# Converting the weights in place over their raw words, with four raw buffers instead of two and two

## The chip, the core and the metric

The kernel runs on one core of a Trainium2 chip. The metric is the device time of one execution in microseconds (us), shown as a median of several runs.

## The reference

Attention with a linear bias and a window feeds two feed-forward layers. Cut to what matters:

```python
scores = scale * np.matmul(q, k.transpose(0, 1, 3, 2))      # batch 4, heads 8, seq 576, head_dim 64
scores = np.where(mask, scores + bias[None], -1000000000.0) # mask: 0 <= rel < 128
...                                                         # softmax
x = np.matmul(attn, v)          # reshaped to (2304, 512)
h = x @ w_in                    # layer 1, d_ff = 2048
g = h * np.clip(h + 3.0, 0.0, 6.0) / 6.0
x = g @ w_out
r = np.maximum(x @ w_in2, 0.0)  # layer 2, weights of its own
g = s * (r * r) + b
out = g @ w_out2
```

The four weight matrices are handed over as 64-bit floats, so each weight comes to the core as two 32-bit words, a low and a high one, side by side.

## The kernel before, in words

The 2304 tokens are eight groups (t = 0 to 7) of 256 or 320 for layer 1, and six groups (t = 8 to 13) of 384 for layer 2. The hidden dimension of 2048 is 16 slices f of 128. A `Step` (t, f) is a first product `h` (L575, 12 matmuls), an activation on ScalarE and VectorE (`relu` L588, `product` L592 or L596, `hi` L605 or L607, `lo` L612 or L614), and a second product `o` (L633 in layer 1, L647 in layer 2). Every matrix operand is kept as two parts, a rounded `hi` and a rest `lo`.

The order of the work is written by hand: `at(slot, rank, fn)` puts each piece into a slot, and all slots are issued in order, so each engine and the sync queue (SP) work through their instructions in that order. A step takes two slots.

`Half` converts the weights. There are 32 halves for each layer, two for each f: the `w_in` part and the `w_out` part. A half with slot s is

- `load` (slot s - 3): one transfer of 512 KB on the sync queue (L168) into a raw tile of 128 x 1024 words; `l` and `h` are its even and odd words, so each is a view of 512 words with a step of 8 bytes;
- `high` (slot s): ScalarE scales the high words into a PSUM bank (L181) and the low words into `q` (L182);
- `sign` (slot s): VectorE shifts the PSUM bank (L186) and joins it with the sign of `h` into `z` (L189);
- `add` (slot s + 1): GpSimd adds `z` and `q` into `q` (L195);
- `hi` (slot s + 2): ScalarE rounds `q` into the weights' tile (L203);
- `lo` (slot s + 3): VectorE writes the rest beside it (L207).

`z` and `q` are the two dense halves of a tile `zq` of 1024 words. The raw tile comes from one of two places. Either it has the tag `raw` (two buffers of 4 KB a partition, and `zq` has two more of its own, given out in `high`), or it is one half of a "stage", a tile of 2048 words in memory that is free at the time, whose other half is the `zq`. In layer 1 the stages are the tiles of the weights 12 to 15, which are filled last; in layer 2 the stage is one tile of the input pool (tag x1), with one buffer. In layer 2 the halves take two raw buffers and the stage in turn. A raw tile of the tag `raw` is last read in `sign`, a stage in `lo`. The outputs `y` of layer 1's groups use the tag `raw` too, and so does a small tile `tmp` at the start.

The halves of layer 1 are planned six slots ahead of their first use, beside the attention of the later groups, whose loads (L280, L286) stand in the same sync queue. The halves of layer 2 are planned 1.74 slots apart from six slots behind the start of t = 7, the last group of layer 1.

Of the kernel before, what the change touches and what calls it, by code (L numbers as in the profile page):

```python
# [8 lines left out]
F32 = mybir.dt.float32  # L9
F32R = mybir.dt.float32r  # L10
I32 = mybir.dt.int32
U32 = mybir.dt.uint32
AF = mybir.ActivationFunctionType
ALU = mybir.AluOpType
PSUM = bass.MemoryType.PSUM

P = 128
# [5 lines left out]
def tile_alibi_window_attention_moe_moe2(  # L23
# [14 lines left out]
    nc = tc.nc  # L38
    B, H, S, D = dims
    T, DM = out.shape  # L40
    NF = w1.shape[0]
# [4 lines left out]
    N1 = max(SIZES1)  # L46
# [5 lines left out]
    wpool = ctx.enter_context(tc.tile_pool(name="wpool", bufs=1))  # L52
    raww = ctx.enter_context(tc.tile_pool(name="raww", bufs=1))
    xpool = ctx.enter_context(tc.tile_pool(name="xpool", bufs=1))
# [6 lines left out]
    nt1 = len(SIZES1)  # L61
# [40 lines left out]
    b_sb = const.tile([P, 1], F32, name="b_sb")  # L102

    def constants():
        tmp = raww.tile([P, P], F32, tag="raw", bufs=2, name="tmp")
        nc.gpsimd.iota(own, pattern=[[-1, P]], base=0, channel_multiplier=1)
        nc.vector.tensor_copy(rel0, own)
        nc.vector.tensor_scalar(
            out=rel2[:, :P], in0=rel0, scalar1=float(P), scalar2=None, op0=ALU.add
        )  # L110
        nc.vector.memset(tmp, 0.0)
        lower = dict(compare_op=ALU.is_ge, base=0, pattern=[[-1, P]], channel_multiplier=1)
        upper = dict(compare_op=ALU.is_ge, base=-1, pattern=[[1, P]], channel_multiplier=-1)
        nc.gpsimd.affine_select(out=tmp, in_=tmp, fill=float(P), **lower)
        nc.vector.tensor_tensor(out=rel, in0=rel0, in1=tmp, op=ALU.add)
        nc.gpsimd.affine_select(out=rel0, in_=rel0, fill=BIG, **lower)
        nc.gpsimd.affine_select(out=rel2[:, :P], in_=rel2[:, :P], fill=BIG, **upper)
        nc.vector.tensor_scalar(
            out=own, in0=tmp, scalar1=-1.0 / P, scalar2=1.0, op0=ALU.mult, op1=ALU.add
        )  # L120
        make_identity(nc, ident)
        nc.sync.dma_start(out=s_sb, in_=s_in.to_broadcast([P, 1]))
        nc.sync.dma_start(out=b_sb, in_=b_in.to_broadcast([P, 1]))
# [4 lines left out]
    def bank(name):  # L128

        nonlocal nbank  # L130
        free = 4 if slot < FIRST else 2 if slot < hslot[1, 0] else 0
        nbank += 1
        k = nbank % (3 + free)
        if k < free:
            return ps_o.tile([P, 512], F32, tag=f"o{3 - k}", name=name)
        return ps_w.tile([P, 512], F32, tag="a", bufs=3, name=name)
# [4 lines left out]
    class Half:  # L141
# [17 lines left out]

        def load(self):  # L160
            if self.stage is None:
                raw = raww.tile([P, 2 * DM], I32, tag="raw", bufs=2, name=f"raw{self.id}")
            else:
                pool, tag = self.stage
                t = pool.tile([P, 4 * DM], I32, tag=tag, name=f"stage{self.id}")
                raw, self.zq = t[:, : 2 * DM], t[:, 2 * DM :]
            src = (w1 if self.layer == 1 else w2)[self.f].bitcast(I32)
            nc.sync.dma_start(out=raw, in_=src[:, 2 * self.i * DM : 2 * (self.i + 1) * DM])  # L168
            raw = raw.rearrange("p (c w) -> p c w", w=2)
            self.l, self.h = raw[:, :, 0], raw[:, :, 1]  # L170

        def high(self):

            if self.stage is None:
                self.zq = raww.tile([P, 2 * DM], I32, tag="zq", bufs=2, name=f"zq{self.id}")
            self.z, self.q = self.zq[:, :DM], self.zq[:, DM:]
            if self.layer == 1:
                self.zp = bank(f"z{self.id}")
            else:
                self.zp = ps_w.tile([P, 512], F32, tag="h", name=f"z{self.id}")  # L180
            nc.scalar.activation(self.zp, self.h.bitcast(F32), AF.Copy, scale=2.0**-112)  # L181
            nc.scalar.activation(self.q, self.l.bitcast(U32), AF.Copy, scale=2.0**-29)  # L182

        def sign(self):
            z = self.zp.bitcast(I32)
            nc.vector.tensor_scalar(  # L186
                out=z, in0=z, scalar1=3, scalar2=None, op0=ALU.logical_shift_left
            )
            nc.vector.scalar_tensor_tensor(  # L189
                out=self.z, in0=self.h, scalar=-(2**31), in1=z,  # L190
                op0=ALU.bitwise_and, op1=ALU.bitwise_or,
            )

        def add(self):
            nc.gpsimd.tensor_tensor(out=self.q, in0=self.z, in1=self.q, op=ALU.add)  # L195

        def hi(self):
            if (self.layer, self.f) not in wt:
                wt[self.layer, self.f] = wpool.tile(
                    [P, 2, 2 * DM], F32R, tag=f"w{self.f}", name=f"w{self.layer}_{self.f}"  # L200
                )
            w = wt[self.layer, self.f]
            nc.scalar.activation(w[:, 0, self.c], self.q.bitcast(F32), AF.Copy)  # L203

        def lo(self):
            w = wt[self.layer, self.f]
            nc.vector.tensor_tensor(  # L207
                out=w[:, 1, self.c], in0=self.q.bitcast(F32), in1=w[:, 0, self.c].bitcast(F32),
                op=ALU.subtract,
            )  # L210

# [3 lines left out]
    xtag = ["x0", "x1", "x2"] + [f"x{(i + 1) % 2}" for i in range(3, nt1)]  # L215
# [331 lines left out]
    class Step:  # L547
# [61 lines left out]
        def lo(self):  # L609
            hi = self.g[:, 0].bitcast(F32)  # L610
            if self.layer == 1:
                nc.vector.tensor_tensor(out=self.g[:, 1], in0=self.a, in1=hi, op=ALU.subtract)  # L612
            else:
                nc.vector.scalar_tensor_tensor(  # L614
                    out=self.g[:, 1], in0=self.a, scalar=b_sb, in1=hi,
                    op0=ALU.add, op1=ALU.subtract,
                )
# [37 lines left out]
        def end(self):  # L655
            t = self.t
            if self.layer == 1:
                if t == nt1 - 1:
                    whole = xpool.tile([P, CC, N1], F32, tag=xtag[t], name=f"y{t}")
                for e in range(0, CC, 2):  # L660
                    if t == nt1 - 1:
                        y = whole[:, e : e + 2]
                    else:
                        y = raww.tile([P, 2, N1], F32, tag="raw", bufs=2, name=f"y{t}_{e}")
                    y = y[:, :, : self.n]
                    nc.scalar.activation(y[:, 0], acc[t][e], AF.Copy, scale=1.0 / 6.0)
                    nc.vector.tensor_scalar(
                        out=y[:, 1], in0=acc[t][e + 1], scalar1=1.0 / 6.0, scalar2=None,
                        op0=ALU.mult,
                    )  # L670
                    nc.sync.dma_start(out=x2d[t][:, e : e + 2], in_=y)
                return
            for tb in range(N2 // P):
                y = late["p"].tile([P, DM], F32, tag="y2", bufs=3, name=f"y{t}_{tb}")
                if tb % 2 == 0:
                    nc.scalar.activation(y, acc[t][tb], AF.Copy)
                else:
                    nc.vector.tensor_copy(y, acc[t][tb])
                r0 = (t - nt1) * N2 + tb * P
                nc.sync.dma_start(out=out[r0 : r0 + P, :], in_=y)  # L680
# [29 lines left out]
            eng.tensor_tensor(out=x[:, 1], in0=raw, in1=x[:, 0].bitcast(F32), op=ALU.subtract)  # L710


    k = 0
    for f in range(NF):
        for i, s in enumerate((hslot[0, f], oslot[0, f])):
            room = [None] * 2 + [(wpool, f"w{i}") for i in range(max(12, f + 3), NF)]
            Half(1, f, i, room[k % len(room)]).plan(s - 6)
            k += 1
    last = hslot[nt1 - 1, 0]
    room = (None, None, (xpool, xtag[nt1 - 2]))  # L720
    for k in range(2 * NF):
        f, i = divmod(k, 2)
        s = max(last + 6 + int(1.74 * k), oslot[nt1 - 1, f])
        Half(2, f, i, room[k % 3]).plan(s)
    for u in units:
        if u.g == 0:
            u.plan(u.h)
# [15 lines left out]
    at(last, 0, late_pool)  # L743
    at(-1, 23, lambda: warm_up(5))
    at(-3, 0, constants)

    with tc.manual_schedule():
# [58 lines left out]
```

## Time and profile before

| | us |
|---|---|
| median of three runs | 970.63 |
| lowest and highest | 966.11, 972.07 |
| profiled execution | 970.56 |
| its span, first to last instruction | 968.4 |
| TensorE busy | 944.5 (98%) |
| VectorE busy | 542.8 (56%) |
| ScalarE busy | 464.4 (48%) |
| GpSimd busy | 288.1 (30%) |

PE is TensorE, DVE is VectorE, ACT is ScalarE, POOL is GpSimd, SPq is the sync queue that issues the transfers. L207 is line 207 of the kernel before. A share of the whole span is a mean over stages: layer 1 with attention (to about 500 us), the conversion of layer 2's weights (about 500 to 624 us) and the rest of layer 2.

### The profile page before, as it was taken

The page shows a single profiled execution, that of the slowest core. Times are in us where ns is not written, and L with a number is a line of the kernel's source. Part 1 is how long each engine was busy: PE and PEld are TensorE (multiplying, and loading weights), DVE is VectorE, ACT ScalarE, POOL GpSimd, SP SyncE. Part 2 cuts the span into 40 slices and gives each one's busy share as a digit, 9 for nine tenths or more (in the row PEclk, how much of TensorE's full clock was granted, in tenths as well). Part 3 has the DMA queues.
Part 4 walks back from the last instruction along what each step waited for, and adds up shares of the span by engine and source line. Part 5 has one row for each costly group of instructions (what it writes and reads, how often), then busy time and mean ns, then how long its engine had stood idle before and what let it go on. Part 6 is the DMA issues. An engine that isn't in the chain of part 4 may idle for free.

```text
span 968.4 us, 16289 instructions
## 1 busy us (share of the span) xinstructions
PE 944.5 (98%) x5978; PEld 867.7 (90%) x5978; DVE 542.8 (56%) x1334; ACT 464.4 (48%) x1201; POOL 288.1 (30%) x544
## 2 busy tenths in 40 slices
PE   8998999999999999999999999899999999999998
PEld 5688889999999999999998877799999999999997
DVE  5999995555555555455359999833323323333322
ACT  4878885555554444444247666433223323223322
POOL 5645783345544444443114533200000000000000
PEclk6599999999999999999999999999999999999999
DMA  6263542222222121220034453120110200200000
GB/s 244 82 202 118 182 154 60 94 72 96 75 93 61 56 87 61 72 84 5 1 136 163 141 175 136 66 66 1 35 31 1 66 1 1 66 0 1 34 1 33
DMA packets 34383, 73.92 MB, mean 76 GB/s; under 512 B 4352, under 2 KB 13568, under 8 KB 34304
## 3 DMA queue, kind: packets, MB, share of 16 engines
q1 hardware_dynamic: 34304, 72.89, 22.7%
q8 instruction: 47, 0.77, 0.3%
q14 instruction: 32, 0.26, 0.1%
HBM read 63.44 MB, written 9.44 MB: 75 GB/s over the span
## 4 chain that ended last, share of the span: by engine, by line
PE 77%; DVE 11%; issue 3%; DMA 3%; ACT 3%; POOL 1%; SPq 0%; POOLq 0%; ACTq 0%; DVEq 0%
PE h L575 34%; PE o L647 18%; PE o L633 15%; DVE w L207 3%; PE s L323 3%; DVE z L186 3%; PE v L406 3%; DMA stage<-w 2%; PE s L478 2%; PE t L375 2%; DVE g L612 1%; PE t L517 1%; DVE t L596 1%; ACT z L181 1%; PE v L531 1%
## 5 line engine op out<-in xcount | busy, mean ns | idle before, releaser
L575 PE MATMUL h<-x,w 128*128 128x384 f32 (+2 forms) x2688 | 446.9, 315 | 4.0 <-DVE t L592 3.7
L575 PEld LDWEIGHTS h<-x,w 128*128 128x128 f32 x2688 | 418.6, 190 | 14.3 <-DVE t L592 5.4
L588 ACT ACTIVATE t<-h 128x384 f32<-128x384 f32 (+2 forms) x224 | 99.5, 444 | 365.2 <-PE h L575 364.4
L633 PE MATMUL o<-g,w 128*128 128x256 f32 (+1 forms) x1536 | 231.6, 299 | 3.5 <-DVE g L612 1.8
L647 PE MATMUL o<-w,g 128*128 128x512 f32 x864 | 217.6, 395 | 7.1 <-ACT g L607 5.1
L633 PEld LDWEIGHTS o<-g,w 128*128 128x128 f32 x1536 | 210.0, 189 | 7.1 <-DVE g L612 3.8
L647 PEld LDWEIGHTS o<-w,g 128*128 128x128 f32 x864 | 159.8, 188 | 40.8 <-ACT g L607 7.7
L596 DVE SCALAR_TENSOR_TENSOR t<-t,s_sb 128x384 f32<-128x384 f32 x96 | 64.4, 671 | 171.5 <-ACT t L588 171.5
L391 POOL TENSOR_SCALAR_AFFINE_SELECT W<-F 128x128 f32<-128x128 f32 (+1 forms) x240 | 68.3, 323 | 145.7 <-ACT F L379 142.0
L592 DVE SCALAR_TENSOR_TENSOR t<-t,h 128x256 f32<-128x256 f32 (+1 forms) x128 | 57.7, 451 | 84.2 <-ACT t L588 84.0
L614 DVE SCALAR_TENSOR_TENSOR g<-t,b_sb,g 128x384 fp32r<-128x384 f32 x96 | 65.1, 678 | 54.1 <-ACT g L607 54.0
L612 DVE TENSOR_TENSOR g<-t,g 128x256 fp32r<-128x256 f32 (+1 forms) x128 | 72.8, 569 | 39.2 <-ACT g L605 38.2
L607 ACT ACTIVATE g<-t,b_sb 128x384 fp32r<-128x384 f32 x96 | 59.2, 616 | 65.4 <-DVE t L596 65.2
L195 POOL TENSOR_TENSOR zq<-zq 128x512 int32<-128x512 int32 x40 | 56.8, 1419 | 83.1 <-DVE zq L189 71.8
L605 ACT ACTIVATE g<-t 128x256 fp32r<-128x256 f32 (+1 forms) x128 | 55.9, 437 | 16.1 <-DVE t L592 16.0
L304 POOL TENSOR_TENSOR C<-raw,C 64x448 fp32r<-64x448 f32 (+1 forms) x48 | 50.8, 1058 | 35.7 <-issue 18.3
L366 POOL TENSOR_SCALAR P<-P,st 128x128 f32<-128x128 f32 x128 | 53.7, 435 | 7.0 <-DVE st L360 5.5
L350 ACT ACTIVATE P<-P,st 128x128 f32<-128x128 f32 x128 | 49.6, 391 | 0.0
L339 DVE COPY_PREDICATED s<-own,s 128x128 f32<-128x128 int32 (+1 forms) x112 | 30.8, 275 | 32.2 <-PE s L323 30.5
L195 POOL TENSOR_TENSOR stage<-stage 128x512 int32<-128x512 int32 x24 | 34.0, 1418 | 44.6 <-DVE stage L189 29.3
L186 DVE TENSOR_SCALAR z<-z 128x512 int32<-128x512 int32 x64 | 44.0, 688 | 2.0 <-ACT z L181 1.9
L340 DVE CUSTOM_DVE_ANT_0 P<-s,rel 128x128 f32<-128x128 f32 x128 | 37.1, 290 | 7.7 <-DVE s L339 0.5
(73 smaller groups left out, 808.5 us busy)
## 6 DMA issues: line engine op xcount, KB each, us to landing
raw<-w SPq DMA_DIRECT2D x40, 512.0 KB, 4.8
stage<-w SPq DMA_DIRECT2D x24, 512.0 KB, 4.4
raw<-qk SPq DMA_DIRECT2D x32, 384.0 KB, 3.0
out<-y SPq DMA_DIRECT2D x18, 256.0 KB, 2.3
raw<-qk SPq DMA_DIRECT2D x16, 256.0 KB, 2.6
rv<-v SPq DMA_DIRECT2D x16, 256.0 KB, 3.3
raw<-qkv0p SPq DMA_DIRECT2D x8, 384.0 KB, 7.2
x2d<-y SPq DMA_DIRECT2D x8, 320.0 KB, 3.1
```

The source lines that it names most:

```text
L186: nc.vector.tensor_scalar(out=z, in0=z, scalar1=3, scalar2=None, op0=ALU.logical_shift_left)
L195: nc.gpsimd.tensor_tensor(out=self.q, in0=self.z, in1=self.q, op=ALU.add)
L391: nc.gpsimd.affine_select(out=self.W[:, o : o + r], in_=self.F[:, q : q + r], fill=0.0, base=k - 1, compare_op=ALU.is_ge, pattern=[[s, r]] ...
L575: nc.tensor.matmul(self.ps, lhsT=w[:, wp, cc * P : (cc + 1) * P], rhs=x[:, cc, xp], start=m == 0, stop=m == 3 * CC - 1,)
L588: nc.scalar.activation(self.a, self.ps, AF.Relu, **bias)
L592: nc.vector.scalar_tensor_tensor(out=self.a, in0=self.a, scalar=6.0, in1=self.ps, op0=ALU.min, op1=ALU.mult)
L596: nc.vector.scalar_tensor_tensor(out=self.a, in0=self.a, scalar=s_sb, in1=self.a, op0=ALU.mult, op1=ALU.mult)
L607: nc.scalar.activation(self.g[:, 0], self.a, AF.Identity, bias=b_sb)
L612: nc.vector.tensor_tensor(out=self.g[:, 1], in0=self.a, in1=hi, op=ALU.subtract)
L614: nc.vector.scalar_tensor_tensor(out=self.g[:, 1], in0=self.a, scalar=b_sb, in1=hi, op0=ALU.add, op1=ALU.subtract,)
L633: nc.tensor.matmul(acc[t][d], lhsT=w[:, wp, DM + d * P : DM + (d + 1) * P], rhs=self.g[:, gp], start=f == 0 and i == 0 and (t > 1 or d % 2 ...
L647: nc.tensor.matmul(acc[t][tb], lhsT=self.g[:, gp, tb * P : (tb + 1) * P], rhs=w[:, wp, DM:], start=f == 0 and i == 0, stop=f == NF - 1 and ...
```

## The change

The conversion writes over the raw words. `high` writes its scaled low words over `l`, `sign` writes over `h`, `add` writes over `l`, and `hi` and `lo` read `l`. The tile `zq` is gone, and the tag `raw` has four buffers in place of two. A stage keeps its size of 2048 words, of which the first half is used. The rotation of tiles changes with it: in layer 1 four raw buffers and the stages 12 to 15, in layer 2 four raw buffers and the stage.

```diff
@@ load
-                raw = raww.tile([P, 2 * DM], I32, tag="raw", bufs=2, name=f"raw{self.id}")
+                raw = raww.tile([P, 2 * DM], I32, tag="raw", bufs=4, name=f"raw{self.id}")
             else:
                 pool, tag = self.stage
-                t = pool.tile([P, 4 * DM], I32, tag=tag, name=f"stage{self.id}")
-                raw, self.zq = t[:, : 2 * DM], t[:, 2 * DM :]
+                raw = pool.tile([P, 4 * DM], I32, tag=tag, name=f"stage{self.id}")[:, : 2 * DM]
@@ high
-            if self.stage is None:
-                self.zq = raww.tile([P, 2 * DM], I32, tag="zq", bufs=2, name=f"zq{self.id}")
-            self.z, self.q = self.zq[:, :DM], self.zq[:, DM:]
-            nc.scalar.activation(self.q, self.l.bitcast(U32), AF.Copy, scale=2.0**-29)
+            nc.scalar.activation(self.l, self.l.bitcast(U32), AF.Copy, scale=2.0**-29)
@@ sign
-                out=self.z, in0=self.h, scalar=-(2**31), in1=z,
+                out=self.h, in0=self.h, scalar=-(2**31), in1=z,
@@ add
-            nc.gpsimd.tensor_tensor(out=self.q, in0=self.z, in1=self.q, op=ALU.add)
+            nc.gpsimd.tensor_tensor(out=self.l, in0=self.h, in1=self.l, op=ALU.add)
@@ hi
-            nc.scalar.activation(w[:, 0, self.c], self.q.bitcast(F32), AF.Copy)
+            nc.scalar.activation(w[:, 0, self.c], self.l.bitcast(F32), AF.Copy)
@@ lo
-                out=w[:, 1, self.c], in0=self.q.bitcast(F32), in1=w[:, 0, self.c].bitcast(F32),
+                out=w[:, 1, self.c], in0=self.l.bitcast(F32), in1=w[:, 0, self.c].bitcast(F32),
@@ the plan of layer 1
-            room = [None] * 2 + [(wpool, f"w{i}") for i in range(max(12, f + 3), NF)]
-            Half(1, f, i, room[k % len(room)]).plan(s - 6)
+            j = next(j for j in room if j is None or j >= f + 3)   # room = [None] * 4 + [12, ..., 15]
+            room.remove(j)
+            room.append(j)
+            Half(1, f, i, None if j is None else (wpool, f"w{j}")).plan(s - 6)
@@ the plan of layer 2
-    room = (None, None, (xpool, xtag[nt1 - 2]))
+    room = (None, None, None, None, (xpool, xtag[nt1 - 2]))
-        Half(2, f, i, room[k % 3]).plan(s)
+        Half(2, f, i, room[k % 5]).plan(s)
```

## Rows read from the trace of the kernel before

**Rows 1.** The page's table of busy us, share and instructions.

```profile
PE 944.5 (98%) x5978; PEld 867.7 (90%) x5978; DVE 542.8 (56%) x1334; ACT 464.4 (48%) x1201; POOL 288.1 (30%) x544
```

**Rows 2.** Windows: length, then PE, PEld, DVE, ACT, POOL busy; clock, DMA.

```profile
60.00:140.00 80.00, 73.21 (x578) 68.08 (x578) 76.50 (x173) 64.61 (x161) 53.62 (x62) 1.00 0.53 171
...
500.00:640.00 140.00, 129.16 (x702) 115.02 (x701) 122.68 (x165) 87.72 (x170) 52.73 (x36) 1.00 0.41 136
640.00:960.00 320.00, 320.00 (x1609) 290.15 (x1608) 104.78 (x173) 94.81 (x176) 0.00 (x0) 1.00 0.06 18
```

**Rows 3.** Waits from 500 to 640 us: total us, times, longest.

```profile
ACT z L181 <- DMA stage<-w: 5.6, 6, 1.7
...
DVE z L186 <- ACT z L181: 1.6, 2, 1.0
```

**Rows 4.** Waits from 60 to 140 us.

```profile
ACT z L181 <- DMA raw<-w: 0.9, 1, 0.9
```

**Rows 5.** Waits of the sync queue, 500 to 640, then 60 to 140 us.

```profile
SPq L168 <- DVE w L207: 70.3, 9, 10.1
...
SPq L280 <- DVE qY L299: 50.1, 9, 13.3
```

**Rows 6.** Timeline around one load into the stage: start, us, instruction.

```profile
520.57 0.68 DVE L207 TENSOR_TENSOR w<-stage,w 128x512 fp32r<-128x512 f32 x1
...
521.28 0.33 SPq L168 DMA_DIRECT2D stage<-w  x1
...
525.49 0.64 ACT L181 ACTIVATE z<-stage 128x512 f32<-128x512 f32 x1 [1.38 <-DMA stage<-w]
526.06 0.64 ACT L182 ACTIVATE stage<-stage 128x512 int32<-128x512 uint32 x1
526.16 0.70 DVE L186 TENSOR_SCALAR z<-z 128x512 int32<-128x512 int32 x1 [1.03 <-ACT z L181]
...
526.89 0.69 DVE L189 SCALAR_TENSOR_TENSOR stage<-stage,z 128x512 int32<-128x512 int32 x1
...
527.11 2.02 PE L633 MATMUL o<-g,w 128*128 128x320 f32 x12 [1.08 <-ACT g L605]
```

**Rows 7.** Groups of instructions by shape: busy us, mean ns of one.

```profile
L195 POOL TENSOR_TENSOR zq<-zq 128x512 int32<-128x512 int32 x40 | 56.8, 1419 | 83.1 <-DVE zq L189 71.8 <-ACT t L588 9.0 <-ACT w L203 1.2
...
L304 POOL TENSOR_TENSOR C<-raw,C 64x448 fp32r<-64x448 f32 x32 | 37.0, 1157 | 28.0 <-issue 14.9 <-POOL P L366 12.7
...
L592 DVE SCALAR_TENSOR_TENSOR t<-t,h 128x320 f32<-128x320 f32 x64 | 31.0, 484 | 52.0 <-ACT t L588 52.0
...
L189 DVE SCALAR_TENSOR_TENSOR zq<-raw,z 128x512 int32<-128x512 int32 x40 | 27.5, 688 | 1.4
L592 DVE SCALAR_TENSOR_TENSOR t<-t,h 128x256 f32<-128x256 f32 x64 | 26.7, 417 | 32.2 <-ACT t L588 32.1
L182 ACT ACTIVATE zq<-raw 128x512 int32<-128x512 uint32 x40 | 26.4, 659 | 0.0
...
L203 ACT ACTIVATE w<-zq 128x512 fp32r<-128x512 f32 x40 | 25.1, 627 | 7.8 <-POOL zq L195 7.8
...
L304 POOL TENSOR_TENSOR C<-raw,C 64x256 fp32r<-64x256 f32 x16 | 13.8, 861 | 7.7 <-POOL P L366 3.5 <-issue 3.4
```

**Rows 8.** Timelines of VectorE and GpSimd: first and last long instructions of each stage.

```profile
39.71 1.73 DVE L207 TENSOR_TENSOR w<-zq,w 128x512 fp32r<-128x512 f32 x1
...
146.34 0.96 DVE L612 TENSOR_TENSOR g<-t,g 128x256 fp32r<-128x256 f32 x1
...
502.63 1.79 DVE L207 TENSOR_TENSOR w<-zq,w 128x512 fp32r<-128x512 f32 x1
...
527.81 1.33 POOL L195 TENSOR_TENSOR stage<-stage 128x512 int32<-128x512 int32 x1 [1.92 <-ACT w L203]
527.90 1.79 DVE L207 TENSOR_TENSOR w<-zq,w 128x512 fp32r<-128x512 f32 x1
...
621.54 1.78 DVE L207 TENSOR_TENSOR w<-zq,w 128x512 fp32r<-128x512 f32 x1
```

More of the change, by code (lines that the diff above doesn't have):

```diff
@@ L104, in constants @@
     def constants():
-        tmp = raww.tile([P, P], F32, tag="raw", bufs=2, name="tmp")
+        tmp = raww.tile([P, P], F32, tag="raw", bufs=4, name="tmp")
         nc.gpsimd.iota(own, pattern=[[-1, P]], base=0, channel_multiplier=1)
@@ L663, in end @@
                     else:
-                        y = raww.tile([P, 2, N1], F32, tag="raw", bufs=2, name=f"y{t}_{e}")
+                        y = raww.tile([P, 2, N1], F32, tag="raw", bufs=4, name=f"y{t}_{e}")
                     y = y[:, :, : self.n]
@@ L710, in split @@
             eng.tensor_tensor(out=x[:, 1], in0=raw, in1=x[:, 0].bitcast(F32), op=ALU.subtract)
-    k = 0
+    room = [None] * 4 + list(range(12, NF))
     for f in range(NF):
         for i, s in enumerate((hslot[0, f], oslot[0, f])):
-            room = [None] * 2 + [(wpool, f"w{i}") for i in range(max(12, f + 3), NF)]
-            Half(1, f, i, room[k % len(room)]).plan(s - 6)
-            k += 1
+            j = next(j for j in room if j is None or j >= f + 3)
+            room.remove(j)
+            room.append(j)
+            Half(1, f, i, None if j is None else (wpool, f"w{j}")).plan(s - 6)
     last = hslot[nt1 - 1, 0]
-    room = (None, None, (xpool, xtag[nt1 - 2]))
+    room = (None, None, None, None, (xpool, xtag[nt1 - 2]))
     for k in range(2 * NF):
```

## The prediction

> **What bounds the kernel now.** I read the busy table first, then the windows, then the waits inside the two stages that the windows single out. TensorE is busy for 944.5 of the 968.4 us span [rows 1], so little beyond TensorE's own idle time can be won. The windows show where that idle time is [rows 2]. From 640 to 960 us TensorE has none. It has 80 - 73.21 = 6.8 us from 60 to 140 us, where the weights of layer 1 are converted beside the attention, and 140 - 129.16 = 10.8 us from 500 to 640 us, where the weights of layer 2 are converted. In both, VectorE is nearly full: 76.50 of 80 us, and 122.68 of 140 us, the last 16 of which lie behind the last conversion. So in these two stages VectorE sets the pace. The change touches only what happens there, and a gain has to come out of VectorE's own idle or stalled time.
>
> VectorE has two kinds of loss in layer 2. The first is the load. The stage tile has one buffer, so a load into it waits on the sync queue for the `lo` of three halves before: the queue waited 70.3 us for that in 9 cases [rows 5]. One instance in full [rows 6]: `lo` L207 starts at 520.57 and takes 0.68, the load is issued at 521.28, ScalarE starts the half (L181) at 525.49, having waited 1.38 us for the data, and VectorE's shift L186 starts at 526.16 after 1.03 us of idleness. There are six such waits, 5.6 us in sum, and VectorE's share in them is 1.6 us in two [rows 3]. The second loss is larger. A VectorE instruction with two inputs in SBUF that begins while GpSimd runs `add` (L195) lasts until the add is done: L207 took 1.79 us against 0.68 while an add ran from 527.81 [rows 6, 8]. Taking as stalled what lasts 0.15 us or more over its unstalled time, I count 26 stalls in the 32 halves of layer 2, nearly all of 1.0 to 1.1 us, from 502.63 to 621.54, and 14 in layer 1, from 39.71 to 146.34 [rows 8]. 40 stalls of about 1 us: this is what the change can make worse.
>
> **The load, part by part.** Buffers: two raw and two `zq` tiles of 4 KB a partition become four raw tiles, so the memory is the same. A raw tile is now held until `lo`, three slots longer than until `sign`, but the rotation in layer 2 goes from three to five. The first `lo` of layer 2 is the one at 502.63 and the last but one that at 621.54 [rows 8], so a half takes 118.9 / 30 = 4.0 us. A load may therefore go out about 2 x 4.0 = 7.9 us sooner than a stage load does now, and the worst lateness is 1.7 us [rows 3]. In layer 2 no attention load stands in the sync queue, so the loads can use this. The gain is bounded from both sides: at least VectorE's 1.6 us of idleness, at most ScalarE's 5.6 us. I take 1.6, because VectorE is full otherwise: where ScalarE waited and VectorE did not go idle, VectorE was still on earlier work.
>
> In layer 1 ScalarE waited only 0.9 us for a raw load [rows 4]. There the sync queue is held by the attention loads L280, 50.1 us in 9 cases, which wait for VectorE's L299 [rows 5]. The loads of weights keep their places behind them, so I cost this at nothing. At the start some loads go out earlier, since eight buffers are empty; nobody waits for them, so nothing there either. The `y` tiles share the raw tag and get four buffers; TensorE does not wait for them in layer 1's steady part, where it has no idle time.
>
> **The in-place operations.** No instruction is added or removed. Of a half's seven operations, 64 times over, five keep their size and get words 8 bytes apart: L182 now also writes so, L189 also writes so, L195 reads twice and writes so, L203 and L207 each read one operand so. What the trace shows of such words is reading. L182 reads them at 659 ns against 627 ns for the dense L203, and it also converts an integer; L189 reads them at 688 ns, as long as L186 beside it, which reads none (0.69 and 0.70) [rows 6, 7]. So I take 0 for reads on ScalarE and VectorE. Strided writes, and any strided operand on GpSimd, have no row. Bounds: for VectorE, if every second word costs as if it were written, L592's 484 - 417 = 67 ns for 64 elements gives 512 x 1.05 = 0.54 us for each L189, x 32 = 17 us in layer 2 and as much again in layer 1; from below 0. For GpSimd the two shapes of L304 give (1157 - 861) / 192 = 1.54 ns an element, so 512 words skipped cost up to 0.79 us on top of 1.42; from below 0 [rows 7]. I take 0 for all, by the nearest rows, which are L182 and L189 on the very same words. A gain from striding is excluded, as no operation does less; but the time at which an add starts against VectorE's order can shift, and three stalls more or fewer are about 3 us either way.
>
> GpSimd is the least certain. The trace has no strided GpSimd row to judge by. [...]
>
> **A new order.** `h` and `l` lie in one tile, word by word. Should L189's write of `h` be ordered behind L182's write of `l`, ScalarE's L182 must end first. In the tightest case, where VectorE waits for ScalarE, L182 starts at 526.06, takes 0.64 and ends at 526.70, and L189 starts at 526.89 [rows 6]: 0.19 us of cover, so it costs nothing. Without cover (a slower L182) VectorE's whole queue stands behind L189, the steps' L592, L596 and L612 and TensorE after them; each 0.1 us over would be 3.2 us in layer 2.
>
> **Sum.** 970.56 (the profiled execution; its span plus 2.2 us around it; the median of the runs is 970.63, so they stand level) - 1.6 = **969.0 us**. With 5.6 us of gain or three stalls fewer it is 964, with three stalls more or a little stride cost 974.
>
> **Rivals.** First, slower: strided words make GpSimd's add longer by x. Each stall lasts until the add is done, so VectorE loses 40x in the two stages that it bounds, and the time is 969.0 + 40x: x = 0.28 us (an add of 1.70 instead of 1.42) passes 1% over the median, 0.79 gives 1000.6. For it: the add has two reads and a write, all strided, and GpSimd shows no such row, which is why the chance is not small. Against: ScalarE and VectorE read these words at the dense rate. [...]
>
> VectorE's strided write (L189) is the same kind of rival with a lower chance, since its strided read is free: 0.54 us each, 969.0 + 34 = 1003 at its bound.
>
> Second, faster: the late loads hold up TensorE and not VectorE alone. ScalarE works in order, and behind the late L181 of 525.49 stood the `hi` (L605) for which TensorE waited 1.08 us at 527.11 [rows 6]. If all idle time of TensorE in layer 2 came from this, it would be 970.6 - 10.8 = 959.8 us. Against: six late loads for 32 halves, and most of TensorE's waits end on ScalarE after a stalled VectorE instruction.
>
> Third, it does not do what it says: the loads still come late, because the queue works in order and raw tiles are freed only at `lo`. Then nothing changes: 970.6. Against: 7.9 us of lead.
>
> **How the numbers follow.** Forecast 58%, still late 12%, faster rival 8%, a longer add 17%, a longer L189 5%. About 1% (9.7 us) is what a measurement of this kernel tells from no change; before, the runs lie from 966.1 to 972.1. So faster by over 1% 8%, slower by over 1% 22%, within 70%. The forecast's own range is 964 to 974. To leave out no more than 2 in 10 the range takes in the forecast, two more us of stalls below it, and the slower rival up to x = 0.4, that is 985; the faster rival (8%), about half of the slower one (8%) and most of the longer L189 (3%) stay outside: **962 to 985**.
>
> **What would show it.** Right: no wait of ScalarE's L181 for a load from 500 to 640 us; loads issued five halves after the tile's last use; L189 at 0.69, unstalled L207 at 0.68, L195 near 1.42, L182 near 0.66; TensorE's idle time there smaller by one to three us. Wrong: L195 above 1.7 with VectorE's stalls longer by the same; L189 above 0.8; VectorE waiting at L189 for L182; or 26 stalls become many more or many fewer.

## The result, and the profile after

The changed kernel takes **959.33 us** (median of 4 runs, 957.75 to 961.14) against 970.62 us (median of 4, 966.11 to 972.07): a ratio of 0.989, with a 95% interval of 0.9868 to 0.9912. It is 1.1% faster, and the prediction (969.0, range 962 to 985) missed it. The profiled execution took 958.67 us, 956.9 of them span.

The busy table of the page after, us, share of the span and instructions, beside [rows 1]:

```profile
PE 938.5 (98%) x5978; PEld 865.6 (90%) x5978; DVE 532.3 (56%) x1334; ACT 465.9 (49%) x1201; POOL 270.4 (28%) x544
```

As many instructions as before run on each engine, but GpSimd works 17.7 us less and VectorE 10.5 us less. So some instructions have become shorter, which the prediction had excluded. The windows say where, in the columns of [rows 2]:

```profile
60.00:140.00 80.00, 74.34 (x586) 69.27 (x587) 74.92 (x176) 66.46 (x166) 50.28 (x66) 1.00 0.47 147
500.00:640.00 140.00, 134.86 (x737) 122.35 (x736) 116.34 (x166) 88.93 (x170) 41.94 (x35) 1.00 0.40 129
```

From 500 to 640 us VectorE is busy 122.68 - 116.34 = 6.3 us less for one instruction more, and TensorE 134.86 - 129.16 = 5.7 us more. From 60 to 140 us TensorE has won only 1.1 us. The groups of the conversion by shape (whole span; busy us, mean ns of one | idle time before them), beside [rows 7], show which instruction it is:

```profile
L191 POOL TENSOR_TENSOR raw<-raw 128x512 int32<-128x512 int32 x47 | 54.5, 1159 | 106.8 <-DVE raw L185 44.4 <-DMA raw<-w 31.2 <-ACT t L584 18.2
L185 DVE SCALAR_TENSOR_TENSOR raw<-raw,z 128x512 int32<-128x512 int32 x47 | 32.4, 689 | 1.6
L199 ACT ACTIVATE w<-raw 128x512 fp32r<-128x512 f32 x47 | 31.4, 669 | 4.4 <-POOL raw L191 4.1
L178 ACT ACTIVATE raw<-raw 128x512 int32<-128x512 uint32 x47 | 31.4, 668 | 0.0
```

L191 is the add (L195 before). Its mean fell from 1419 to 1159 ns, though the words of its inputs and of its output now lie 8 bytes apart. The other three kept their time within 1 to 42 ns: L185 688 to 689, L178 659 to 668, L199 627 to 669.

The timeline (start, us, instruction) shows what that does to VectorE, where [rows 8] had L207 at 1.79 us beside an add of 1.33:

```profile
505.95 0.69 DVE L203 TENSOR_TENSOR w<-raw,w 128x512 fp32r<-128x512 f32 x1
...
506.17 1.36 POOL L191 TENSOR_TENSOR raw<-raw 128x512 int32<-128x512 int32 x1 [2.21 <-DVE raw L185]
506.56 1.33 DVE L608 TENSOR_TENSOR g<-t,g 128x320 fp32r<-128x320 f32 x1
...
509.45 1.04 POOL L191 TENSOR_TENSOR stage<-stage 128x512 int32<-128x512 int32 x1 [1.91 <-DVE stage L185]
509.53 1.50 DVE L203 TENSOR_TENSOR w<-raw,w 128x512 fp32r<-128x512 f32 x1
...
512.68 0.69 DVE L203 TENSOR_TENSOR w<-stage,w 128x512 fp32r<-128x512 f32 x1
```

L203 (the `lo`) takes 0.69 us alone and 1.50 when it begins 0.08 us behind an add of 1.04; it ends 0.54 us after that add. An add can be held up in turn: the one of 506.17 begins while the L203 of 505.95 is under way, and takes 1.36. By the prediction's own count (0.15 us or more over the unstalled time) layer 2 has 26 stalls as before, but they cost 20.92 us in place of 27.33. The other part is the load. Among the waits from 500 to 640 us (total us, times, longest), that of ScalarE's first step for a load, 5.6 us in [rows 3], is gone. The first row below is the only one that still names a weight load; it stands ahead of an add on another tile than that load's, on an engine that is idle for 98 of the 140 us. The second row is what is left ahead of ScalarE's step.

```profile
POOL raw L191 <- DMA stage<-w: 1.2, 1, 1.2
...
ACT z L177 <- DVE raw L185: 0.9, 2, 0.7
```

and among the sync queue's own waits of the same stretch, the one that answers to [rows 5] is

```profile
SPq L167 <- DVE w L203: 79.6, 26, 6.2
```

The queue now waits 26 times for a tile's last reader, and ScalarE waits for no weight load.

**Where the 11.5 us of span went**, by the starts of the same `h` matmuls (L575 before, L571 after; the 224 groups of 12 are counted from 0):

```
start of group      0      4      28      112     116     148    end of span
before            39.09  63.33  151.84  487.30  501.38  644.05   968.43
after             38.37  60.38  148.40  483.86  497.94  632.55   956.94
```

Layer 2's stage (groups 116 to 148) went from 142.67 to 134.61, so 8.06 us came from there. Groups 4 to 28 gave 0.5, groups 0 to 4 gave 2.2, and 0.7 lies ahead of group 0. What lies behind group 148 takes as long as before (324.38 and 324.39).

The two stretches of layer 1 differ in what bounds them. These are their windows, before:

```profile
39.09:63.33 24.24, 23.36 (x145) 19.14 (x143) 23.89 (x52) 19.07 (x50) 11.99 (x16) 0.76 0.46 151
63.33:151.84 88.51, 82.60 (x656) 77.71 (x657) 81.84 (x195) 70.89 (x182) 60.29 (x75) 1.00 0.47 150
```

and after:

```profile
38.37:60.38 22.01, 20.82 (x144) 17.06 (x143) 21.67 (x51) 19.37 (x50) 10.26 (x15) 0.94 0.50 159
60.38:148.40 88.02, 82.74 (x656) 77.67 (x657) 80.30 (x195) 71.17 (x182) 54.54 (x75) 1.00 0.44 138
```

From group 0 to 4 VectorE has no time left in either (idle 0.35 and 0.34 us). Its stalls there, counted in the same way over all of its instructions, fell from 5.3 us in 6 to 2.9 in 4, and the stretch shrank by as much. From group 4 to 28 they fell from 7.3 us in 16 to 5.2 in 10, but VectorE's idle time rose from 6.7 to 7.7 us, and the stretch shrank by 0.5 only.

### The profile page after: what moved, and what is told of

It reads as the page before. It is cut to its first block, busy times and chain, and to the rows that moved or that the text cites. A ratio compares the mean times of both kernels' runs of the same rounds, so it can differ in the third digit from the quotient of the medians.

```text
span 956.9 us, 16309 instructions
## 1 busy us (share of the span) xinstructions
PE 938.5 (98%) x5978; PEld 865.6 (90%) x5978; DVE 532.3 (56%) x1334; ACT 465.9 (49%) x1201; POOL 270.4 (28%) x544
## 4 chain that ended last, share of the span: by engine, by line
PE 78%; DVE 9%; ACT 4%; DMA 3%; issue 3%; POOL 1%; SPq 0%; ACTq 0%; POOLq 0%; DVEq 0%
PE h L571 34%; PE o L643 18%; PE o L629 16%; PE s L319 3%; PE v L402 3%; DMA raw<-w 2%; DVE w L203 2%; DVE z L182 2%; PE t L371 2%; PE s L474 2%; ACT z L177 1%; DVE t L592 1%; DVE raw L185 1%; PE t L513 1%; ACT w L199 1%
## 5 line engine op out<-in xcount | busy, mean ns | idle before, releaser
L571 PE MATMUL h<-x,w 128*128 128x384 f32 (+2 forms) x2688 | 445.9, 315 | 4.3 <-DVE t L588 4.2
L571 PEld LDWEIGHTS h<-x,w 128*128 128x128 f32 x2688 | 417.6, 189 | 15.1 <-DVE t L588 6.3
L592 DVE SCALAR_TENSOR_TENSOR t<-t,s_sb 128x384 f32<-128x384 f32 x96 | 63.1, 658 | 171.5 <-ACT t L584 171.5
L608 DVE TENSOR_TENSOR g<-t,g 128x256 fp32r<-128x256 f32 (+1 forms) x128 | 70.5, 551 | 40.2 <-ACT g L601 39.4
L191 POOL TENSOR_TENSOR raw<-raw 128x512 int32<-128x512 int32 x47 | 54.5, 1159 | 106.8 <-DVE raw L185 44.4
L182 DVE TENSOR_SCALAR z<-z 128x512 int32<-128x512 int32 x64 | 44.1, 689 | 1.1 <-ACT z L177 0.7
L203 DVE TENSOR_TENSOR w<-raw,w 128x512 fp32r<-128x512 f32 x47 | 42.6, 907 | 0.0
```

Of the source, the lines that this page charges most:

```text
L182: nc.vector.tensor_scalar(out=z, in0=z, scalar1=3, scalar2=None, op0=ALU.logical_shift_left)
L203: nc.vector.tensor_tensor(out=w[:, 1, self.c], in0=self.l.bitcast(F32), in1=w[:, 0, self.c].bitcast(F32), op=ALU.subtract,)
L571: nc.tensor.matmul(self.ps, lhsT=w[:, wp, cc * P : (cc + 1) * P], rhs=x[:, cc, xp], start=m == 0, stop=m == 3 * CC - 1,)
L592: nc.vector.scalar_tensor_tensor(out=self.a, in0=self.a, scalar=s_sb, in1=self.a, op0=ALU.mult, op1=ALU.mult)
```

## The experiments

Eight kernels. A to D ran on one chip (before: median 970.03), E to H on another (before: 971.73). How long TensorE stays at half of its clock at the start differs from run to run (from 20 to 40 us the granted clock was 0.50 in the traces of before, after, A and B, and 0.83 in those of C, F and H), so "layer 2" below is the time from group 116 to group 148 in the one profiled execution of each, which lies behind that.

**A, a_interleave: the layout without the buffers.** The kernel before, with its two `zq` tiles and its rotation, but `q` and `z` lie word by word in `zq`:

```diff
-            self.z, self.q = self.zq[:, :DM], self.zq[:, DM:]
+            zq = self.zq.rearrange("p (c w) -> p c w", w=2)
+            self.q, self.z = zq[:, :, 0], zq[:, :, 1]
```

> The kernel before with one edit: z and q of a half are the odd and even words of zq in place of its two dense halves, so ScalarE, VectorE and GpSimd work on words 8 bytes apart as in the changed kernel, but not over the raw words, and buffers and loads stay as before. Theory 1 (the gain in layer 2 is a shorter add, through VectorE's stalls): the add takes about 1.16 us on average in place of 1.42, the loads of the stage still come late (some 5 us of waits of ScalarE), and the time falls by 26 x 0.26 = 6.8 us in layer 2 and about 1 us in layer 1, to 962 to 965 us. Theory 2 (the loads hold up TensorE): no gain, 969 to 972 us, whatever the add takes. Theory 3 (the add is shorter because it works in place over its tile of raw words, not because of the step): the add stays at 1.42 us and the time at 969 to 972 us.

Measured: 961.99 us, ratio 0.9915 (0.9881 to 0.9949). Layer 2 took 136.39 us, 6.3 less than before. A's add among the groups by shape:

```profile
L196 POOL TENSOR_TENSOR zq<-zq 128x512 int32<-128x512 int32 x40 | 46.7, 1168 | 86.2 <-DVE zq L190 67.0 <-ACT t L589 13.6 <-ACT g L608 2.5
```

Its wait for loads from 500 to 640 us:

```profile
ACT z L182 <- DMA stage<-w: 4.2, 5, 1.2
```

And its window of that stretch:

```profile
500.00:640.00 140.00, 133.35 (x731) 120.63 (x731) 117.28 (x167) 88.74 (x171) 43.72 (x35) 1.00 0.41 135
```

The add is as short as after (1168 ns), the loads are still late (4.2 us in 5 waits), and the 26 stalls cost 20.7 us. So the short add needs neither the raw tile nor the buffers, and alone it is worth most of the gain.

**B, b_split_stage: the earlier load without the layout.** The kernel before, but layer 2's stage tile is taken once and kept, so that its raw half is free for the next load once the sign of three halves before has read it:

```diff
-                t = pool.tile([P, 4 * DM], I32, tag=tag, name=f"stage{self.id}")
+                if self.layer == 1 or "t" not in kept:
+                    kept["t"] = pool.tile([P, 4 * DM], I32, tag=tag, name=f"stage{self.id}")
+                t = kept["t"]
```

> The kernel before with one edit: in layer 2 the stage is one tile that is kept, so that a load into its raw half waits for the last reader of that half (the sign, L189, of three halves before) and not for lo. z and q stay dense. Loads of layer 2 come three slots earlier, all else is as before. Theory 1: no late load of the stage in layer 2 any more, the add still 1.42 us, and the time falls by VectorE's 1.6 us of idleness to at most 3 us: 967.5 to 969 us. Theory 2 (late loads hold up TensorE): the time falls by about 8 us to 962 us.

Measured: 968.50 us, ratio 1.0001 (0.9985 to 1.0017). B's window of layer 2:

```profile
500.00:640.00 140.00, 130.46 (x707) 116.42 (x706) 122.12 (x164) 86.84 (x169) 52.21 (x35) 1.00 0.41 135
```

Its only wait for a load in that stretch:

```profile
POOL stage L200 <- DMA xr<-x2d: 0.7, 1, 0.7
```

And its add among the groups by shape:

```profile
L200 POOL TENSOR_TENSOR zq<-zq 128x512 int32<-128x512 int32 x40 | 56.8, 1419 | 83.4 <-DVE zq L194 73.0 <-ACT t L593 9.0 <-ACT w L208 0.8
```

No weight load is late any more, yet TensorE wins only 1.3 us here and layer 2 takes 141.09, 1.6 us less. That is read from one trace; the ratio shows no gain, and its interval allows one of 1.5 us at most. The 26 stalls cost 27.27 us, as before. This refutes the faster rival, that the late loads hold TensorE, whose 959.8 us was near the result. A and B together make 6.3 + 1.6 = 7.9 of after's 8.06 us, and after is 1.8 us shorter there than A, which lacks only the buffers and the work in place.

**C, c_inplace_shallow: the layout with too few buffers.** The changed kernel with two raw buffers and the rotations of before:

```diff
-                raw = raww.tile([P, 2 * DM], I32, tag="raw", bufs=4, name=f"raw{self.id}")
+                raw = raww.tile([P, 2 * DM], I32, tag="raw", bufs=2, name=f"raw{self.id}")
...
-    room = (None, None, None, None, (xpool, xtag[nt1 - 2]))
+    room = (None, None, (xpool, xtag[nt1 - 2]))
```

> The changed kernel with the buffers undone: in place over the raw words, but two raw buffers and the rotation of before, so that in layer 2 every load waits for lo of three halves before. Theory 1: the add about 1.16 us; the stalls shrink by 0.26 us each (about 7 us), but every load and not every third now comes 1 to 2 us late, which VectorE feels: 965 to 975 us. Theory 2: all loads late, so much slower than before: 980 us or more. Theory 3 (in place makes the add short): the add 1.16 us here and 1.42 us with interleaved words in a tile of their own.

Measured: 973.43 us, ratio 1.0043 (1.0023 to 1.0062). Layer 2 took 138.66 us, 4.0 less than before, but groups 4 to 28 took 100.57 against 88.51. The window of layer 1's stage in C:

```profile
60.00:140.00 80.00, 66.09 (x502) 60.62 (x501) 64.70 (x152) 57.67 (x145) 44.32 (x57) 0.99 0.40 136
```

ScalarE's wait for loads in the same stretch, where [rows 4] had 0.9 us:

```profile
ACT z L177 <- DMA raw<-w: 12.9, 6, 3.7
```

VectorE is idle for 15 of 80 us, 11.5 of them in 7 waits of its first step (L182) for ScalarE. A raw load goes out as a `lo` ends: one at 94.13 us, behind an L203 that began at 93.41 and took 0.69. The time lies where the first theory had it, but that theory looked for the loss in layer 2, and it came in layer 1. So with two raw buffers working in place costs 12.1 us there, since it holds a raw tile until `lo`, and layer 2 is 2.3 us longer than with A's layout alone; the two freed buffers give both back, and 1.8 us more in layer 2.

**D, d_layouts: which of the add's operands shortens it.** The kernel before, each half with one of eight layouts in turn, and each add on a line of its own; only the durations of the adds are read, from one execution.

```diff
+            self.v = (2 * self.f + self.i) % 8
+            self.z, self.q, self.r = [
+                (lower, upper, upper), (zq[:, :, 1], zq[:, :, 0], zq[:, :, 0]),
+                (lower, upper, lower), (self.h, upper, upper), (lower, self.l, self.l),
+                (self.h, self.l, self.l), (self.h, self.l, upper), (lower, upper, self.l),
+            ][self.v]
```

> A measurement of the add alone, inside the kernel before: the halves go through eight layouts in turn, each with its add on a line of its own: (0) z, q dense, out over q, as before; (1) z, q interleaved in zq; (2) dense, out over z; (3) z in place over h with a step, q dense; (4) z dense, q and out in place over l; (5) all in place, as in the changed kernel; (6) both inputs in place over h and l, out dense; (7) inputs dense, out over l. Shortest add of each: 1.26 us for layout 0 and 1.03 for layout 5 by the two kernels. If the step of the two inputs decides, layouts 1, 5 and 6 take 1.03 us and 0, 2, 4 (in part), 7 take 1.26. If the step of the output decides, 1, 4, 5 and 7 take 1.03. If it is in which memory the operands stand (in place), 1 takes 1.26 and 5 takes 1.03.

Measured, per line of the add (count: least/median/longest ns, and when). In this order: dense; interleaved in `zq`; only `z` in place; only `q` and the output in place; all in place; both inputs in place with a dense output; dense inputs with the output in place:

```profile
L208 POOL TENSOR_TENSOR zq<-zq x5: 1264/1294/1537, 23.0 to 590.9; 128x512 int32<-128x512 int32 x5
L210 POOL TENSOR_TENSOR zq<-zq x5: 1035/1154/1353, 33.2 to 595.0; 128x512 int32<-128x512 int32 x5
...
L214 POOL TENSOR_TENSOR zq<-raw,zq x5: 1311/1472/1542, 95.8 to 602.6; 128x512 int32<-128x512 int32 x5
L216 POOL TENSOR_TENSOR raw<-zq,raw x6: 1305/1309/1497, 68.7 to 607.1; 128x512 int32<-128x512 int32 x6
L218 POOL TENSOR_TENSOR raw<-raw x5: 1034/1039/1367, 73.4 to 578.3; 128x512 int32<-128x512 int32 x5
L220 POOL TENSOR_TENSOR zq<-raw x5: 1038/1268/1357, 43.8 to 617.8; 128x512 int32<-128x512 int32 x5
L222 POOL TENSOR_TENSOR raw<-zq x5: 1291/1451/1622, 54.4 to 621.1; 128x512 int32<-128x512 int32 x5
```

The instances of one layout differ by 0.2 to 0.3 us, as an add can be held up by VectorE (506.17 us above), so the least values are compared. It takes 1.03 to 1.04 us when both inputs are the two words of the pairs, wherever the output goes, and 1.26 to 1.31 otherwise. The output does not matter, and one strided input gains nothing.

**E, e_layouts2: the step, or lying side by side.** As D, with other layouts. In five the inputs are the alternating blocks of one tile, in blocks of `n` words; in two they are steps of 8 bytes in two different tiles.

```diff
+            self.n = [None, None, None, 2, 4, None, 256, None][self.v]
...
+            self.q, self.z = [
+                (even, odd), (even, self.h), (self.l, even), (even, odd),
+                (even, odd), (even, odd), (even, odd), (self.zq[:, DM:], self.zq[:, :DM]),
+            ][self.v]
```

> A second measurement of the add alone inside the kernel before, again eight layouts in turn, each with its add on a line of its own; out is always over q. (0) z and q interleaved word by word in zq; (1) both with a step of 8 bytes, but in two tiles: z in place over h, q in the even words of zq; (2) the same the other way: z in the even words of zq, q in place over l; (3) interleaved in pairs of words, (4) in fours, (6) in blocks of 256; (5) interleaved word by word, with the two inputs exchanged; (7) dense, as before. Layout 0 should repeat 1.03 us and layout 7 1.26 us. If it is the step of both inputs that shortens the add, 1, 2 and 5 take 1.03 us, and 3, 4 and 6 take 1.26 us or a little more. If it is that the two inputs lie side by side, 1 and 2 take 1.26 us, and 3, perhaps 4, 1.03 us.

Measured, in the same form and in this order: alternating words; steps in two tiles, twice; alternating pairs; alternating fours; alternating words with the inputs exchanged; blocks of 256; dense:

```profile
L208 POOL TENSOR_TENSOR zq<-zq x5: 1037/1039/1257, 21.9 to 593.4; 128x512 int32<-128x512 int32 x5
L210 POOL TENSOR_TENSOR zq<-raw,zq x5: 1501/1652/1824, 32.3 to 597.3; 128x512 int32<-128x512 int32 x5
L212 POOL TENSOR_TENSOR raw<-zq,raw x4: 1512/1694/1982, 91.3 to 568.9; 128x512 int32<-128x512 int32 x4
L214 POOL TENSOR_TENSOR zq<-zq x5: 1034/1257/1329, 97.5 to 605.2; 128x512 int32<-128x512 int32 x5
L216 POOL TENSOR_TENSOR zq<-zq x6: 1278/1280/1444, 68.7 to 609.5; 128x512 int32<-128x512 int32 x6
L218 POOL TENSOR_TENSOR zq<-zq x5: 1034/1060/1355, 73.3 to 580.5; 128x512 int32<-128x512 int32 x5
L220 POOL TENSOR_TENSOR zq<-zq x5: 1300/1582/1588, 43.1 to 620.1; 128x512 int32<-128x512 int32 x5
L222 POOL TENSOR_TENSOR zq<-zq x5: 1292/1511/1590, 53.7 to 623.6; 128x512 int32<-128x512 int32 x5
```

It is not the step. With steps of 8 bytes in two places the add is longer, 1.50 us, and that is the slower rival's mechanism, in a layout that the change does not have. What shortens the add is that the two inputs alternate by 4 or 8 bytes; when they alternate by 16 bytes it takes as long as dense (1.28 us against 1.29).

**F, f_square_psum: a stall fewer.** If VectorE instructions with two inputs in SBUF are what an add holds, one with a single input there should not be. The changed kernel, with layer 2's square taking its second factor from PSUM, where the same values still stand:

```diff
-                    out=self.a, in0=self.a, scalar=s_sb, in1=self.a, op0=ALU.mult, op1=ALU.mult
+                    out=self.a, in0=self.a, scalar=s_sb, in1=self.ps, op0=ALU.mult, op1=ALU.mult
```

> The changed kernel with one edit: the square of layer 2 (L592) multiplies the activated values with the product still in PSUM in place of with themselves, which gives the same number, so that this instruction has one input in SBUF and not two. If a stall of VectorE is what the shape of an instruction's inputs makes it (two in SBUF while GpSimd adds), the five or so stalls at L592 of 0.8 us each go, those elsewhere stay, and the time falls by about 4 us, to 955 us. If the stalls are only waits for the result of the add, or pass on to the next instruction, it stays at 959 us.

Measured: **955.63 us**, ratio 0.9833 (0.9806 to 0.9861), which beats both kernels (after's interval begins at 0.9868). The square's group by shape, from 495 to 640 us, first in after:

```profile
L592 DVE SCALAR_TENSOR_TENSOR t<-t,s_sb 128x384 f32<-128x384 f32 x22 | 17.4, 790 | 13.1 <-ACT t L584 13.1
```

then in F:

```profile
L592 DVE SCALAR_TENSOR_TENSOR t<-t,s_sb,h 128x384 f32<-128x384 f32 x23 | 14.0, 609 | 16.0 <-ACT t L584 15.9
```

and F's window of layer 2:

```profile
500.00:640.00 140.00, 137.03 (x749) 125.64 (x748) 111.02 (x164) 87.61 (x168) 40.75 (x34) 1.00 0.39 126
```

The five stalls at L592, 3.99 us in after, are gone: 21 stalls and 16.6 us are left. Unstalled, the square takes 0.61 us either way ((17.4 - 3.99) / 22 in after). Layer 2 takes 131.07 us, 3.5 less than after, and TensorE is busy for 137.03 of 140 us.

Two inputs in SBUF are not the whole condition. In layer 1 of the kernel before, a VectorE instruction on 128 x 2 words with one input in SBUF (L501), which takes 0.16 us at its shortest, is held by an add as well, for 1.26 us:

```profile
32.95 1.26 DVE L501 TENSOR_SCALAR st<-st 128x2 f32<-128x2 f32 x1
```

```profile
32.91 1.27 POOL L195 TENSOR_TENSOR zq<-zq 128x512 int32<-128x512 int32 x1
```

What sets it apart from F's square was not tried.

**G, g_pitch: halves closer together.** If VectorE has time left, layer 2's halves could follow each other faster. The changed kernel with

```diff
-        s = max(last + 6 + int(1.74 * k), oslot[nt1 - 1, f])
+        s = max(last + 6 + int(1.6 * k), oslot[nt1 - 1, f])
```

> The changed kernel with layer 2's halves planned 1.6 slots apart in place of 1.74: if VectorE still sets the pace there, planning them closer moves no work off it and the time stays within 3 us of 959; if the plan held the conversions back, it falls by up to the 5 us that TensorE is still idle in that stage.

Measured: 965.77 us, ratio 0.9930 (0.9902 to 0.9957), slower than after, which neither theory had; layer 2 takes 139.57 us, 5 more. G's `lo` among the groups by shape, from 495 to 640 us (after had 26 at 942 ns):

```profile
L203 DVE TENSOR_TENSOR w<-raw,w 128x512 fp32r<-128x512 f32 x26 | 28.2, 1083 | 0.0
```

G's window of layer 2:

```profile
500.00:640.00 140.00, 130.93 (x718) 118.11 (x718) 117.31 (x166) 89.48 (x171) 43.10 (x36) 1.00 0.41 134
```

The stalls barely rise (27, 21.43 us) but gather on `lo`: 15 of them there, 11.77 us, against 9 and 7.6 in after. VectorE is busy 1.0 us longer, while TensorE loses 3.9 of its 140 us. That the new order costs more than its stalls is measured; which wait carries it was not tried.

**H, h_both: F and G together.** Both edits above.

> Both edits, the square from PSUM and the pitch of 1.6: 953 to 956 us if they add up, a version faster than both kernels; no better than the square alone if VectorE sets the pace.

Measured: 958.90 us, ratio 0.9871 (0.9848 to 0.9894); 23 stalls, 17.3 us; layer 2 135.17. The two do not add up: the closer halves take back 4.1 us of F's layer 2, so F stands.

## Why the prediction was wrong

**The bound** was right in layer 2: from 500 to 640 us VectorE's busy time fell by 6.3 us and TensorE's rose by 5.7; behind 640 us nothing moved. In layer 1 it was not borne out. From group 4 to 28, which is nearly the prediction's stretch of 60 to 140 us, VectorE's stalls fell by 2.1 us in after and by 2.0 in A, but the stretch took 88.02 and 88.94 us against 88.51. VectorE sets the pace ahead of that stretch, from group 0 to 4.

**The load's term, 1.6 us,** agrees with the traces: B, which does only this, shortens layer 2 by 1.6 us, though its ratio does not resolve so little. ScalarE's 5.6 us of waits were worth no more, as they lay mostly beside VectorE's own work.

**The step that failed** is the cost of the in-place add: "I take 0 for all", and above all "A gain from striding is excluded, as no operation does less". The number of words was taken as the only thing that could make an operation shorter, so the bound "from below 0" had no row behind it; every strided row of before had one strided input, and none had two inputs side by side. The add fell from 1419 to 1159 ns in the mean, and 26 stalls of layer 2, each of which waits for its add, fell by (27.33 - 20.92) / 26 = 0.25 us each: 6.4 us that the sum did not have. A gives the same with the layout alone (6.3), D and E show which property it is.

**The mechanism of the slower rival** was right and its sign was open. With x = 1.159 - 1.419 = -0.26 us its own formula, 969.0 + 40x, gives 958.6 us; 959.33 was measured. The prediction carried x from 0 to 0.79 and never below. That the formula comes so near is partly luck. Its 40 stalls of about 1 us are 26 in layer 2, which gave 6.4 us, and 14 in layer 1, from which it expects 3.6 us. But layer 1's are not of that size: L207 has 14 of 0.15 us or more there, 7.8 us in sum, and seven of them are about 0.2 us or less. Groups 4 to 28 gave 0.5 us, and the rest came from groups 0 to 4, where two stalls are gone. That stretch took 24.24 us before and 24.20 in B, 22.01 after and 22.11 in A, and 23.0 to 23.3 in C, F, G and H. VectorE's stalls in it are 5.3 and 5.2 us, 2.9 and 3.0, and 3.7 to 3.8 in C, F and H; in G they are 2.6, but TensorE is never idle there (24.00 of 24 us busy from 40 to 64 us, with 151 matmuls against F's 168). So these 2.2 us come from the add too.

The 0 that the sum took for the add stood on rows of ScalarE and VectorE alone (L182, L189). On GpSimd the runs show it for one strided input, within 0.05 us (1.31 against 1.26), but not for two of them: 1.50 in separate places, 1.03 side by side.

**The faster rival** had almost the right number, 959.8 us, for a reason that B refutes: without a late load TensorE wins 1.3 us from 500 to 640 us, not 10.8.

**It does not do what it says** is refuted too: ScalarE waits for no weight load in layer 2 after. C shows that the concern behind it, raw tiles freed only at `lo`, is real with two buffers (12.9 us of waits in layer 1's stage).

**The other costs at nothing** held: L185 689 ns (688), L178 668 (659), an unstalled L203 0.69 us (0.68). L199 became 42 ns longer, on ScalarE, which has 51 of 140 us idle in layer 2's stage. No wait of VectorE for ScalarE at L185 appeared, so the new order behind L178 costs nothing.

**What stays open:** 11.5 us of span are accounted for as 8.06 + 0.5 + 2.2 + 0.7. The last lies ahead of group 0, where the granted clock differs between the two profiled executions (0.50 against 0.69 from 10 to 20 us), so whether it is the change's is not known. In groups 0 to 4 the clock differs as well (0.76 against 0.94), but B, at 0.93, took as long there as before. What bounds groups 4 to 28 was not tried.

## What to carry to other kernels

"The operation does no less work" does not bound its time from below: when two operands change where they lie relative to each other, an unknown price can be negative, and the range has to be carried to both sides. Where one engine's instruction is held until another's ends, price each stall by the length of the other, and look for the operand that can be read from another place: one factor read from PSUM and not from SBUF gave F another 3.5 us in layer 2. When a rival gives the right time, run it alone before believing it; and buffers that an in-place rewrite frees may only pay for the longer hold that it brings, as C against A and after shows.

## What the runs showed of the hardware

- A GpSimd add of 128 x 512 int32 takes, at its shortest, 1.26 to 1.31 us with both inputs dense, or with one of the two at a step of 8 bytes; 1.50 with both at that step in two places; 1.03 with both in one place, alternating by 4 or 8 bytes; 1.28 alternating by 16. Where the output goes made no difference above 0.03 us (D: with the inputs side by side 1.034 us for an output in place and 1.038 for a dense one, with dense inputs 1.291 and 1.264).
- A VectorE instruction with two inputs in SBUF that began beside such an add did not end before it: L203 took 1.50 us against 0.69 and ended 0.54 us after its add, and all 39 of that kind in after, as all 44 before, ended 0.34 to 0.64 us behind theirs. With one of them in PSUM the square has no such stall (F: 609 ns in the mean against 790), but a 128 x 2 instruction with a single input in SBUF had one (L501, 1.26 us against 0.16). An add that began while an L203 was under way took 1.27 to 1.46 us in after, against 1.03 to 1.04 at its shortest.
- The granted clock of the first 64 us differs between runs of kernels whose start is the same: from 20 to 40 us it was 0.50 in after, with 73 matmuls, and 0.83 in F, with 87; group 4 started at 60.38 and 55.79 us. TensorE had been busy for 7.35 of the first 10 us in after, and for 6.74 in C, where the clock from 20 to 40 us was 0.83 as well. G's rows give 1.00 for that stretch with 72 matmuls, about the count of after at 0.50, so the clock is to be read beside the count.
